# A fused attention and MLP kernel: the last batch's attention in the other direction, MLP weights loaded in other pieces

## The chip, the cores and the metric

One Trainium2 chip, one of its cores. The metric is the device time of one execution in microseconds (us). The kernel before takes 748.22 us, the median of 3 runs (746.31 to 751.43).

## The reference

Three layers follow each other on 4 batches of 768 tokens with 384 channels:

```
state = alpha[t] * state + k[t] v[t]^T ;  y[t] = q[t] state              # gated linear attention, 8 heads of 48
for each of 4 experts e:  a = softmax(causal(q_e k_e^T / 8))             # x = y; q_e, k_e, v_e are x times weights, 64 wide
    out += gate[e] * (a @ v_e) @ wo[e]                                   # gate: softmax over the best two of 4 logits
out + relu(layernorm(out) @ w_ch1) @ w_ch2                               # MLP, 384 -> 1536 -> 384
```

All inputs are fp32. The causal attention of a token block i (128 tokens, i from 0 to 5) looks at i+1 blocks of keys, so the work of a block grows with i.

## The kernel before, in words

The kernel interleaves three strands on the same engines. The **front** (`front`) computes the linear attention in chunks of 128 tokens and the Q, K, V and gates of the second layer. The **attention** of the experts runs in 48 units `u`, listed in `UN`: batch b, token block i, expert pair p, in that order. The **back** (`back`) is the MLP in 12 blocks of 256 tokens: layer norm (`mlp_ln`), transposes (`mlp_tr`), first product (`mlp_1`, 108 matmuls) and second product (`mlp_2`, 72 matmuls).

A loop over the units sets the order: for unit u it issues the transposes of the probabilities (`transp`, L464), the scores two units ahead (`scores`, L432), the product with V (`av`, L487) and, after a pair of units, the output projection (`wout`, L505). Between them, `fill` pulls as much of the front (batches 0 to 2) or of the back (batch 3) as a table of nominal costs says is due. `MB0` (in ns) holds the back's start off by that much nominal work of the last batch. The framework then places the instructions in each engine's own queue, which runs strictly in order.

In `scores`, DVE takes the row maximum (L438 for one half of a wide row, L440 with the causal mask for the rest), ACT makes the exponentials (L442), DVE and POOL make `rr`, the gate over the row sum. In `av`, matmuls of the probabilities with V fill the second 128 columns of a PSUM tile, then two matmuls (L490) spread `rr` over the first 128 columns; ACT copies those (L493, `rb`), DVE multiplies both (L494), ACT and POOL split the result in two parts for `wout`.

The MLP's weights come as 64-bit words (`raw`) and are turned into pairs of fp32r numbers, high and low, by `conv`: a DMA on SP's queue, five operations on DVE (L530 to L534, L544), one on ACT, one on POOL. The first weight is converted in 18 pieces of 256 columns while batches 0 to 2 run, and stored in DRAM (`wsc`). A piece's load waits for a one-element copy on POOL (L526) that reads the latest row maximum; this keeps the load from running far ahead. The load is issued in the same step as the conversion.

At the first unit of the last batch (`u == u3`, unit 36) the front ends and its buffers are freed. `load_mlp(0)` loads the converted first weight, 4.7 MB, from `wsc` by four DMAs of POOL's queue into one tile, in column ranges of the flattened weight. `load_mlp(1)` issues the conversion of all 12 pieces of the second weight (384 columns each, into `w2h` and `w2l`), and `back` starts with the loads of the first two token blocks (`xt`, four DMAs on SP).

Of the kernel before, what the change touches and what calls it, by code (L numbers as in the profile page):

```python
# [11 lines left out]
FR = mybir.dt.float32r  # L12
# [13 lines left out]
MB = 1.0  # L26
MB0 = -15000
TM = 4
# [25 lines left out]
W2 = 384  # L54
PRI = 0
B, H, S, D = 4, 8, 768, 48
DM = H * D
E, HD = 4, 64
DFF = 4 * DM
NSC = S // 128  # L60
KT = DM // 128
# [10 lines left out]
def kernel(ctx: ExitStack, tc: tile.TileContext, akq, vd, wqkv, wo, g_ln, w1, w2, out):  # L72
# [335 lines left out]

    UN = [(b, i, p) for b in range(B) for i in range(NSC) for p in range(2)]
    AA, ATT, OT, RR, M = {}, {}, {}, {}, {}  # L410
# [61 lines left out]
    def av(u):  # L472
# [8 lines left out]
        O = P[:, 128:256]  # L481
        with tc.manual_schedule(engines={mybir.EngineType.PE}):
            for x in range(i + 1):
                for h in range(2):
                    e = 2 * p + h
                    c = 128 * (h * (i + 1) + x)
                    pe.matmul(O[64 * h:64 * h + 64, :], V[:, x, HD * e:HD * e + HD], at[:, c:c + 128],  # L487
                              start=(x == 0), stop=(x == i), skip_group_check=True)
            for h in range(2):
                pe.matmul(P[64 * h:64 * h + 64, :128], rr[:, h:h + 1].to_broadcast([128, 64]), ident, start=True, stop=True,  # L490
                          skip_group_check=True)
        rb = aw.tile([128, 128], F32, name="rb", bufs=2)
# [22 lines left out]
    CW1 = 256  # L515
    NC1 = 3 * DFF // CW1

    def conv(n):
        if n < NC1:
            i, c, cw, p = 0, n, CW1, gw  # L520
        else:
            i, c, cw, p = 1, n - NC1, W2, M["x"]
        cs = slice(cw * c, cw * c + cw)
        raw = p.tile([128, cw, 2], I32, name="raw", bufs=RB)
        if i == 0:
            pool.tensor_copy(raw[0:1, 0, 0:1].bitcast(F32), M["nm"][0:1, 0:1])  # L526
        sp.dma_start(raw.rearrange("p n w -> p (n w)"), (w1, w2)[i][:, 2 * cw * c:2 * cw * (c + 1)])
        a = p.tile([128, cw], I32, name="cva", bufs=CB)
        u = p.tile([128, cw], I32, name="cvu", bufs=CB)
# [18 lines left out]
    def load_mlp(i):  # L548
        if i == 0:
            M["p", 0] = ctx.enter_context(tc.tile_pool(name="mw0", bufs=1))  # L550
            t = M["p", 0].tile([128, 2, 3 * DFF], FR, name="w1hl")
            for c in range(4):
                cs = slice(DFF * 3 // 4 * c, DFF * 3 // 4 * (c + 1))
                pool.dma_start(t[:, :, cs], wsc[:, :, cs])
            for x, n in ((0, "h"), (1, "l")):
                M[f"w1{n}"] = t[:, x].rearrange("p (k c) -> p k c", k=KT)
        else:
# [3 lines left out]
            M["x"] = ctx.enter_context(tc.tile_pool(name="mx", bufs=2))  # L561
            with tc.high_priority(offset=-PRI):
                for c in range(4608 // W2):
                    conv(NC1 + c)

# [51 lines left out]
    def mlp_1(blk, fs):  # L617
        nh, nl = M["n", blk]
        for ff in fs:
            P = psm()[:, :256]  # L620
            c = slice(128 * ff, 128 * ff + 128)
            n = 0
            for w, x in ((M["w1h"], nh), (M["w1l"], nh), (M["w1h"], nl)):
                for k in range(KT):
                    pe.matmul(P, w[:, k, c], x[:, k], start=(n == 0), stop=(n == 8))  # L625
                    n += 1
# [24 lines left out]
    def back():  # L651
        mlp_load(0)
        mlp_load(1)
        mlp_ln(0)
        yield from mlp_tr(0)
        for blk in range(NBLK):
# [7 lines left out]
            if blk + 2 < NBLK:  # L664
                while 256 * (blk + 3) > prog["x"]:
                    yield -1
                mlp_load(blk + 2)
# [42 lines left out]
    for u in range(nu):  # L710
# [13 lines left out]
        if u < u3:  # L724
            ncv = max(0, min(NC1, (NC1 * (u + 1 - CV0)) // (CVU - CV0)))
            while prog["cv"] < ncv:
                conv(prog["cv"])
                prog["cv"] += 1
# [80 lines left out]
```

## Time and profile before

| | |
|---|---|
| median of 3 runs | 748.22 us (746.31 to 751.43) |
| the profiled execution, its own time | 750.77 us |
| its span, first to last instruction | 749.1 us |
| mean granted TensorE clock | 0.973 |
| PE busy | 711.3 us (95%) |
| DVE busy | 448.4 us (60%) |
| ACT busy | 309.2 us (41%) |
| POOL busy | 172.9 us (23%) |

Reading: the span is one execution; 750.77 us is its time as the runs are timed, 1.7 us more than the span. The busy shares are means over very different stretches. From about 472 us on only the MLP is left, and PE runs matmuls back to back; before that the three strands share all engines. A matmul's bar ends when its result is out, which is later than the time at which the next can start, so PE's busy share is too high wherever matmuls of different kinds follow each other.

### The profile page before, as it was taken

What the parts mean: (1) busy time and instruction counts of PE and PEld (TensorE: products, weight loads), DVE (VectorE), ACT (ScalarE), POOL (GpSimd) and SP (SyncE); (2) the same over time, 40 slices, a digit from 0 to 9 for tenths busy, and PEclk for the clock granted to TensorE, in tenths of its full rate; (3) what the DMA queues carried; (4) which work ended last, traced back from release to release, by engine and by line L of the source; (5) the groups of instructions that cost most, each with busy time, mean ns of one, the idle gap of its engine ahead of it and who ended that gap; (6) DMA issues with size and microseconds to landing.
All of it is one profiled execution on the core that took longest, in us unless ns stands there. A gap on an engine that the chain in (4) does not pass through costs nothing.

```text
span 749.1 us, 16235 instructions
## 1 busy us (share of the span) xinstructions
PE 711.3 (95%) x6520; PEld 641.5 (86%) x6520; DVE 448.4 (60%) x1241; ACT 309.2 (41%) x879; POOL 172.9 (23%) x284
## 2 busy tenths in 40 slices
PE   7489799989989899999899999999999999999998
PEld 6478678778868788878677889999999999999997
DVE  6766778767887787766578873254245325433521
ACT  3333455444555555545567553232223123212310
POOL 4643344343554234321233220000000000000000
PEclk9698999989989999999999999999999999999999
DMA  8122423233323612211923311001101100110100
GB/s 338 71 96 90 138 85 135 83 117 122 121 97 96 208 49 92 79 40 55 326 100 95 86 33 62 15 31 43 43 11 33 43 22 22 43 43 12 32 22 22
DMA packets 28380, 60.87 MB, mean 81 GB/s; under 512 B 2961, under 2 KB 16785, under 8 KB 28305
## 3 DMA queue, kind: packets, MB, share of 16 engines
q1 hardware_dynamic: 18864, 45.68, 18.5%
q10 hardware_dynamic: 8352, 9.44, 3.5%
q0 software_dynamic: 1088, 4.72, 1.7%
q8 instruction: 51, 0.84, 0.5%
q14 instruction: 25, 0.20, 0.1%
HBM read 45.67 MB, written 14.16 MB: 80 GB/s over the span
## 4 chain that ended last, share of the span: by engine, by line
PE 59%; DVE 4%; DMA 3%; ACT 2%; POOL 2%; issue 2%; ACTq 0%; POOLq 0%; DVEq 0%
PE F L625 21%; PE F L642 20%; PE F L487 4%; PE F L464 3%; PE F L432 3%; DMA raw<-in_w_dram 2%; PE F L304 2%; PE F L505 2%; PE F L606 1%; PE F L318 1%; DMA ld<-in_akq_dram 1%; ACT A L442 1%; PE F L490 1%; DVE gt L199 1%; PE F L263 1%
## 5 line engine op out<-in xcount | busy, mean ns | idle before, releaser
L629 ACT ACTIVATE hh<-F 128x256 fp32r<-128x256 f32 x144 | 55.0, 384 | 199.9 <-PE F L625 198.8
L625 PE MATMUL F<-nh,w1hl 128*128 128x256 f32 x864 | 129.4, 284 | 0.5 <-ACT nh L610 0.5
L625 PEld LDWEIGHTS F<-nh,w1hl 128*128 128x128 f32 x864 | 114.9, 191 | 2.5 <-issue 1.0
L642 PE MATMUL F<-w2h,hh 128*128 128x384 f32 x288 | 98.1, 341 | 0.0
L642 PE MATMUL F<-w2l,hh 128*128 128x384 f32 x288 | 97.1, 337 | 0.0
L642 PE MATMUL F<-w2h,hl 128*128 128x384 f32 x288 | 96.8, 336 | 0.0
L630 DVE SCALAR_TENSOR_TENSOR hl<-F,hh 128x256 fp32r<-128x256 f32 x144 | 60.0, 420 | 54.2 <-ACT hh L629 54.1
L442 ACT ACTIVATE A<-F,nm 128x384 f32<-128x384 f32 (+4 forms) x128 | 68.5, 542 | 53.5 <-DVE nm L440 43.0
L646 DVE TENSOR_TENSOR xt<-F,xt 128x384 f32<-128x384 f32 x24 | 13.4, 558 | 113.0 <-PE F L642 113.0
L625 PE MATMUL F<-nl,w1hl 128*128 128x256 f32 x432 | 75.7, 283 | 0.0
L487 PE MATMUL F<-at,V 128*64 128x128 f32 x672 | 62.7, 287 | 2.0 <-DVE rb L494 0.9
L625 PEld LDWEIGHTS F<-nl,w1hl 128*128 128x128 f32 x432 | 62.2, 192 | 0.2 <-issue 0.2
L464 PE MATMUL F<-ident,A 128*128 128x128 f32 x336 | 56.1, 289 | 3.1 <-DVE rb L494 2.4
L487 PEld LDWEIGHTS F<-at,V 128*64 128x64 f32 x672 | 41.8, 138 | 18.9 <-issue 7.0
L642 PEld LDWEIGHTS F<-w2h,hh 128*128 128x128 f32 x288 | 54.2, 188 | 0.4 <-issue 0.4
L642 PEld LDWEIGHTS F<-w2l,hh 128*128 128x128 f32 x288 | 54.2, 188 | 0.3 <-DVE at L469 0.2
L642 PEld LDWEIGHTS F<-w2h,hl 128*128 128x128 f32 x288 | 54.1, 188 | 0.0
L464 PEld LDWEIGHTS F<-ident,A 128*128 128x128 f32 x336 | 38.4, 145 | 13.2 <-issue 5.7
L221 PE MATMUL F<-ld 48*128 48x128 f32 x384 | 36.6, 302 | 11.2 <-issue 7.8
L221 PEld LDWEIGHTS F<-ld 48*128 48x128 f32 x384 | 29.3, 197 | 17.3 <-issue 12.0
L206 POOL TENSOR_TENSOR ld<-ld,gt 128x512 f32<-128x512 f32 (+1 forms) x26 | 30.2, 1165 | 59.7 <-DVE gt L199 27.9
L199 DVE TENSOR_TENSOR_SCAN gt<-ld,hot 128x516 f32<-128x516 f32 (+1 forms) x26 | 31.1, 1204 | 16.1 <-DMA ld<-in_akq_dram 12.9
(185 smaller groups left out, 1425.6 us busy)
## 6 DMA issues: line engine op xcount, KB each, us to landing
ld<-in_akq_dram SPq DMA_DIRECT2D x24, 770.0 KB, 5.3
vb<-in_vd_dram SPq DMA_DIRECT2D x24, 256.0 KB, 2.8
raw<-in_w_dram SPq DMA_DIRECT2D x18, 256.0 KB, 2.7
wsc<-whl ACTq DMA_DIRECT2D x18, 256.0 KB, 2.4
xs<-xo ACTq DMA_DIRECT2D x24, 192.0 KB, 1.9
w1hl<-wsc POOLq DMA_DIRECT2D x4, 1152.0 KB, 13.8
raw<-in_w_dram SPq DMA_DIRECT2D x12, 384.0 KB, 3.3
xt<-xs SPq DMA_DIRECT2D x24, 192.0 KB, 2.5
```

The costliest lines, as they stand in the source:

```text
L199: dve.tensor_tensor_scan(gt[:, js].rearrange("p j t -> p (j t)"), al[:, 129 * j0:129 * j1], hot[:, js].rearrange("p j t -> p (j t)"), 0.0, ...
L206: (dve if GQ else pool).tensor_tensor(q[:, js], q[:, js], gt[:, js, 1:], op=OP.mult)
L221: pe.matmul(P[h][:, j], k[r, j], q[r, j], start=True, stop=True)
L304: pe.matmul(P[:, mt % 2], wt[:, k, cs], x[:, k], start=(n == 0), stop=(n == 8))
L432: pe.matmul(P[h][x], qt[rs[h], p, qs], kt[rs[h], p, pw * x:pw * x + pw], start=(n == 0), stop=(n == 2), skip_group_check=True)
L442: act.activation(A[h][:, pw * x:pw * x + pw], t, AF.Exp, bias=nm[:, h:h + 1], scale=1.0 if x < npc - 1 else -1.0, accum_out=dn2[:, h, x:x ...
L464: pe.transpose(P[:, 128 * n:128 * n + 128], A[h][:, 128 * x:128 * x + 128], ident)
L487: pe.matmul(O[64 * h:64 * h + 64, :], V[:, x, HD * e:HD * e + HD], at[:, c:c + 128], start=(x == 0), stop=(x == i), skip_group_check=True)
L625: pe.matmul(P, w[:, k, c], x[:, k], start=(n == 0), stop=(n == 8))
L629: act.activation(hh, P, AF.Relu)
L630: dve.scalar_tensor_tensor(hl, P, 0.0, f(hh), op0=OP.max, op1=OP.subtract)
L642: pe.matmul(P, x[:, o], w[:, ff], start=(ff == 0 and n == 0), stop=(ff == KF - 1 and n == 2))
```

## The change

- The last batch's units run from block 5 down to block 0 instead of from 0 up to 5. Batches 0 to 2 are as before.
- `MB0` goes from -15000 to -10000: the back starts earlier in nominal work.
- In `av` the two matmuls that spread `rr` are issued ahead of the product with V.
- `conv` is cut in two: `conv_load(n)` asks for a piece, `conv(n)` converts it. The load of piece n+1 is issued ahead of the conversion of piece n.
- The second weight's 12 pieces are no longer issued all at unit 36; `CR = 5` issues them at 2.5 pieces a unit over units 37 to 41.
- The `xt` loads of the first two token blocks are issued ahead of the second weight's first piece.
- The first weight goes into four tiles, each with the 384 columns that three steps of `mlp_1` need of all row groups; a DMA's contiguous run is 1536 bytes instead of 4608.

```diff
-MB0 = -15000
+MB0 = -10000
-PRI = 0
+CR = 5
-    UN = [(b, i, p) for b in range(B) for i in range(NSC) for p in range(2)]
+    UN = [(b, i, p) for b in range(B) for i in (range(NSC) if b < B - 1 else reversed(range(NSC))) for p in range(2)]
...
         with tc.manual_schedule(engines={mybir.EngineType.PE}):
+            for h in range(2):
+                pe.matmul(P[64 * h:64 * h + 64, :128], rr[:, h:h + 1].to_broadcast([128, 64]), ident, start=True, stop=True,
+                          skip_group_check=True)
             for x in range(i + 1):
...
-            for h in range(2):
-                pe.matmul(P[64 * h:64 * h + 64, :128], rr[:, h:h + 1].to_broadcast([128, 64]), ident, start=True, stop=True,
-                          skip_group_check=True)
...
+    def conv_load(n):
+        i, c, cw, p = piece(n)
         raw = p.tile([128, cw, 2], I32, name="raw", bufs=RB)
         if i == 0:
             pool.tensor_copy(raw[0:1, 0, 0:1].bitcast(F32), M["nm"][0:1, 0:1])
         sp.dma_start(raw.rearrange("p n w -> p (n w)"), (w1, w2)[i][:, 2 * cw * c:2 * cw * (c + 1)])
+        M["raw", n] = raw
+
+    def conv(n):
+        i, c, cw, p = piece(n)
+        cs = slice(cw * c, cw * c + cw)
+        raw = M.pop(("raw", n))
...
-            t = M["p", 0].tile([128, 2, 3 * DFF], FR, name="w1hl")
+            src = wsc.rearrange("p x (k c) -> p (x k) c", k=KT)
             for c in range(4):
-                cs = slice(DFF * 3 // 4 * c, DFF * 3 // 4 * (c + 1))
-                pool.dma_start(t[:, :, cs], wsc[:, :, cs])
...
+                t = M["p", 0].tile([128, 2, KT, DFF // 4], FR, name=f"w1hl{c}")
+                pool.dma_start(t.rearrange("p x k c -> p (x k) c"), src[:, :, DFF // 4 * c:DFF // 4 * (c + 1)])
+                M["w1", c] = t
...
-            with tc.high_priority(offset=-PRI):
-                for c in range(4608 // W2):
-                    conv(NC1 + c)
+            mlp_load(0)
+            mlp_load(1)
+            conv_load(NC1)
...
-                while 256 * (blk + 3) > prog["x"]:
+                while (256 * (blk + 3) if blk < 3 * S // 256 - 2 else B * S) > prog["x"]:
...
             while prog["cv"] < ncv:
-                conv(prog["cv"])
+                n = prog["cv"]
+                if n + 1 < NC1:
+                    conv_load(n + 1)
+                conv(n)
                 prog["cv"] += 1
+            if u == 0:
+                conv_load(0)
+        else:
+            nc2 = min(NC2, (u - u3) * CR // 2)
+            while prog["cv"] < NC1 + nc2:
+                n = prog["cv"]
+                if n + 1 < NC1 + NC2:
+                    conv_load(n + 1)
+                conv(n)
                 prog["cv"] += 1
```

SP's queue where the last batch begins, before (512 columns of `raw` are a piece of the first weight, 768 one of the second; `xt` is a token block):

```order
L112 DMA vb_89<-in_vd_dram 128x512
L527 DMA raw<-in_w_dram 128x512 x5
L527 DMA raw<-in_w_dram 128x768 x2
L573 DMA xt<-xs 128x384 x4
L527 DMA raw<-in_w_dram 128x768 x10
L647 DMA out_dram<-xt 128x384 x2
```

and now:

```order
L112 DMA vb_89<-in_vd_dram 128x512
L527 DMA raw<-in_w_dram 128x512 x4
L578 DMA xt<-xs 128x384 x4
L527 DMA raw<-in_w_dram 128x768 x12
L653 DMA out_dram<-xt 128x384 x2
```

The four `xt` loads have moved ahead of the second weight's first two pieces, and the last piece of the first weight is asked for earlier, ahead of rows that are not shown.

DVE's queue at the scores of unit 34 (L438 and L440 with 384 columns), before:

```order
L438 TENSOR_REDUCE mx_5018<-F 128x1 x2
L440 ISA F,nm<-F,cmask,mx_5018 128x384
L440 ISA nm 128x1
L440 ISA F,nm<-F,cmask,mx_5018 128x384
L440 ISA nm 128x1
L530 TENSOR_SCALAR cva<-raw 128x384
L531 SCALAR_TENSOR_TENSOR cva<-raw,cva 128x384
L532 TENSOR_SCALAR cvu<-cva 128x384
L534 SCALAR_TENSOR_TENSOR cvu<-raw,cvu 128x384
L338 TENSOR_REDUCE rank<-gt__4997 128x8
L446 SCALAR_TENSOR_TENSOR den<-dn_5019 128x2
```

and now (L590 is the layer norm's statistics of `xt`):

```order
L438 TENSOR_REDUCE mx_5018<-F 128x1 x2
L590 BN_STATS bs<-xt 128x6
L440 ISA F,nm<-F,cmask,mx_5018 128x384
L440 ISA nm 128x1
L440 ISA F,nm<-F,cmask,mx_5018 128x384
L440 ISA nm 128x1
L590 BN_STATS bs<-xt 128x6
L591 BN_AGGR mv<-bs 128x2 x2
L592 TENSOR_SCALAR ve<-mv 128x2
L446 SCALAR_TENSOR_TENSOR den<-dn_5019 128x2
L449 RECIPROCAL den<-den 128x2
```

The conversion of the second weight's first piece stood behind unit 34's masks; its place is now behind the first half of unit 35's, and two of the four statistics of `xt` stand among unit 34's operations, the first ahead of its masks.

PE's queue at the back's first transposes (`ident,xn`), before (L432 with 320 columns are the scores of a block 4, of unit 44):

```order
L505 MATMUL F<-OWH,ol 128x384
L464 MATMUL F<-ident,A 128x128
L487 MATMUL F<-at,V_1411 64x128 x3
L464 MATMUL F<-ident,A 128x128 x4
L606 MATMUL F<-ident,xn 128x128 x6
L432 MATMUL F<-KH_1409,QH_1407 128x320
```

and now (512 columns: the scores of a block 3, of unit 40):

```order
L484 MATMUL F<-ident,rr 64x128 x2
L490 MATMUL F<-at,V_1414 64x128
L611 MATMUL F<-ident,xn 128x128 x6
L490 MATMUL F<-at,V_1414 64x128 x11
L631 MATMUL F<-nh,w1hl_5329 128x256
L464 MATMUL F<-ident,A 128x128 x4
L631 MATMUL F<-nh,w1hl_5329 128x256
L432 MATMUL F<-KH_1412,QH_1410 128x512 x2
```

Before, the back starts ahead of unit 44's scores, when blocks 0 to 2 of the last batch are done; now it starts ahead of unit 40's, at the product of unit 37, the second of block 5.

## Rows read from the trace of the kernel before

**Rows 1.** The page, busy time of engines: busy us, share, instructions.

```profile
PE 711.3 (95%) x6520; PEld 641.5 (86%) x6520; DVE 448.4 (60%) x1241; ACT 309.2 (41%) x879; POOL 172.9 (23%) x284
```

**Rows 2.** Busy time by stretch; clock, DMA share and GB/s at the end.

```profile
357.00:400.00 43.00, 40.33 (x340) 29.71 (x340) 31.38 (x123) 28.96 (x94) 13.53 (x29) 0.96 0.58 198
400.00:432.00 32.00, 31.33 (x268) 27.06 (x266) 27.51 (x79) 20.76 (x66) 9.67 (x14) 1.00 0.34 93
```

**Rows 3.** The chain of waits, 357 us on: start us, us, what.

```profile
357.05 1.06 PE F L432 x7
...
399.85 0.22 PE F L606 x2
...
432.20 1.06 PE F L642 x6
...
472.85 12.48 PE F L642 x72
485.33 12.94 PE F L625 x108
```

**Rows 4.** The chain's shares by line, stretch 200 to 360 us.

```profile
by line: DMA raw<-in_w_dram 11.6%; PE F L304 9.9%; issue 7.4%; PE F L487 5.4%; PE F L432 5.3%; PE F L318 4.7%; PE F L464 4.2%; DMA ld<-in_akq_dram 4.1%; ACT A L442 3.5%; DVE gt L199 3.3%; PE F L263 2.5%; PE F L221 2.2%; PE F L505 2.1%; POOL
```

**Rows 5.** DVE at L530: the group, then three in time with idle before them.

```profile
L530 DVE TENSOR_SCALAR cva<-raw 128x256 int32<-128x256 int32 x18 | 5.8, 325 | 13.3 <-DMA raw<-in_w_dram 13.2
...
301.50 0.29 DVE L530 TENSOR_SCALAR cva<-raw 128x256 int32<-128x256 int32 x1 [0.93 <-DMA raw<-in_w_dram]
...
312.07 0.29 DVE L530 TENSOR_SCALAR cva<-raw 128x256 int32<-128x256 int32 x1 [1.17 <-DMA raw<-in_w_dram]
...
324.87 0.29 DVE L530 TENSOR_SCALAR cva<-raw 128x256 int32<-128x256 int32 x1 [0.91 <-DMA raw<-in_w_dram]
```

**Rows 6.** Waits of DVE at L494: us in total, times, longest.

```profile
DVE rb L494 <- ACT rb L493: 10.1, 10, 2.5
```

**Rows 7.** DVE in time, where the last batch's loads begin; idle before in brackets.

```profile
358.74 0.62 DVE L440 CUSTOM_DVE_ANT_0 F<-F,cmask,mx 128x384 f32<-128x384 f32 x1
...
363.40 0.36 DVE L530 TENSOR_SCALAR cva<-raw 128x384 int32<-128x384 int32 x1 [3.44 <-DMA raw<-in_w_dram]
...
367.03 0.61 DVE L440 CUSTOM_DVE_ANT_0 F<-F,cmask,mx 128x384 f32<-128x384 f32 x1
...
368.58 0.56 DVE L585 BATCH_NORM_STATS2 bs<-xt 128x6 f32<-128x384 f32 x1 [0.65 <-DMA xt<-xs]
...
376.20 0.56 DVE L585 BATCH_NORM_STATS2 bs<-xt 128x6 f32<-128x384 f32 x1 [1.54 <-DMA xt<-xs]
```

**Rows 8.** PE in time, the same place.

```profile
367.10 0.66 PE L464 MATMUL F<-ident,A 128*128 128x128 f32 x4 [1.90 <-DVE rb L494]
```

**Rows 9.** Issue to landing of the four xt loads, then of the first weight's.

```profile
DMA to landing us min/median/max: 9.6/11.9/15.4
...
DMA to landing us min/median/max: 8.0/13.8/19.5
```

**Rows 10.** ACT and DVE groups of a unit and of a piece, by shape.

```profile
L467 ACT ACTIVATE at<-F 128x512 f32<-128x512 f32 x52 | 31.1, 599 | 5.4 <-PE F L464 4.1 <-DVE smk L225 1.1
L442 ACT ACTIVATE A<-F,nm 128x384 f32<-128x384 f32 x48 | 27.6, 584 | 16.1 <-DVE nm L440 14.2 <-PE F L318 1.4 <-PE F L464 0.4
L442 ACT ACTIVATION_READ_ACCUMULATOR A<-F,nm 128x1 f32 x128 | 25.9, 203 | 0.0
L495 ACT ACTIVATE oh<-rb 128x128 fp32r<-128x128 f32 x48 | 14.8, 308 | 22.5 <-DVE rb L494 22.2 <-ACT at L467 0.2
L493 ACT ACTIVATE rb<-F 128x128 f32<-128x128 f32 x48 | 13.2, 275 | 23.9 <-PE F L490 14.9 <-PE F L221 2.6 <-DVE whl L544 2.4
...
L534 DVE SCALAR_TENSOR_TENSOR cvu<-raw,cvu 128x384 f32<-128x384 uint32 x12 | 7.7, 645 | 0.3
```

**Rows 11.** The chain, PE's pace in two kinds of matmul.

```profile
407.96 0.91 PE F L487 x13
...
426.77 1.05 PE F L505 x6
```

More of the change, by code (lines that the diff above doesn't have):

```diff
@@ L516, with piece @@
     NC1 = 3 * DFF // CW1
[L518 to L523, printed above, removed]
+    NC2 = 3 * DFF // W2
+    def piece(n):
+        return (0, n, CW1, gw) if n < NC1 else (1, n - NC1, W2, M["x"])
+    def conv_load(n):
+        i, c, cw, p = piece(n)
         raw = p.tile([128, cw, 2], I32, name="raw", bufs=RB)
@@ L550, in load_mlp @@
             M["p", 0] = ctx.enter_context(tc.tile_pool(name="mw0", bufs=1))
-            t = M["p", 0].tile([128, 2, 3 * DFF], FR, name="w1hl")
+            src = wsc.rearrange("p x (k c) -> p (x k) c", k=KT)
             for c in range(4):
-                cs = slice(DFF * 3 // 4 * c, DFF * 3 // 4 * (c + 1))
-                pool.dma_start(t[:, :, cs], wsc[:, :, cs])
-            for x, n in ((0, "h"), (1, "l")):
-                M[f"w1{n}"] = t[:, x].rearrange("p (k c) -> p k c", k=KT)
+                t = M["p", 0].tile([128, 2, KT, DFF // 4], FR, name=f"w1hl{c}")
+                pool.dma_start(t.rearrange("p x k c -> p (x k) c"), src[:, :, DFF // 4 * c:DFF // 4 * (c + 1)])
+                M["w1", c] = t
         else:
@@ L620, in mlp_1 @@
             P = psm()[:, :256]
-            c = slice(128 * ff, 128 * ff + 128)
+            t = M["w1", ff // 3]
+            c = slice(128 * (ff % 3), 128 * (ff % 3) + 128)
             n = 0
-            for w, x in ((M["w1h"], nh), (M["w1l"], nh), (M["w1h"], nl)):
+            for w, x in ((t[:, 0], nh), (t[:, 1], nh), (t[:, 0], nl)):
                 for k in range(KT):
@@ L651, in back @@
     def back():
-        mlp_load(0)
-        mlp_load(1)
         mlp_ln(0)
@@ L726 @@
             while prog["cv"] < ncv:
-                conv(prog["cv"])
+                n = prog["cv"]
+                if n + 1 < NC1:
+                    conv_load(n + 1)
+                conv(n)
+                prog["cv"] += 1
+            if u == 0:
[7 more added lines that the diff above has]
+                conv(n)
                 prog["cv"] += 1
```

## The prediction

> **What bounds the kernel now.** I read the page's engine totals first: PE is busy 95% of the span [rows 1], so only what PE loses can be won. From 472.85 us on nothing is lost: 72 matmuls take 12.48 us and 108 take 12.94 us [rows 3], 173 and 120 ns each, one behind the other to the end. No part of the change touches that tail but the order of two weight tiles. So I looked at the stretches before it, by busy time [rows 2], and then at the chain of waits for the moments at which the last batch begins (unit 34's scores, 357.05 us), the back begins (399.85 us), its second product begins (432.20 us) and block 2 begins (485.33 us) [rows 3].
>
> The stretch from 357 to 400 us is the loose one: PE starts only 340 matmuls in 43 us, 126 ns each where many are short products that can follow each other every 70 ns (0.91 us for 13) [rows 2, 11], and no other engine is above 31.4 us [rows 2]. Something waits there that is no engine's throughput. DVE's rows in time show it: unit 34's mask starts at 358.74, then DVE stands 3.44 us for the first piece of the second weight, starts unit 35's mask at 367.03 only, and stands again for `xt` at 368.58 and at 376.20 [rows 7]. PE pays with a hole of 1.90 us [rows 8], and the granted clock of the stretch is 0.96 [rows 2], so part of it ran at the lower of TensorE's two levels. From 400 to 432 us DVE is busy 27.5 of 32 us [rows 2]: there it is the bound.
>
> **The change, part by part.** The sum is made against the profiled execution, 750.8 us, which is 2.55 us above the median of the runs; what it gains is taken off the median of 748.2.
>
> *Pieces of the first weight asked for ahead.* DVE waits 13.2 us for these loads in all [rows 5]; the chain from 200 to 360 us has 11.6% of its time, 18.6 us, on such loads [rows 4], but that is issue to landing, and the load's own time is mostly covered. What removal can give is DVE's idle time where the chain passes. It passes five pieces of the first weight there (and the second weight's first at its end); in three of them DVE stood 0.93, 1.17 and 0.91 us [rows 5], in the other two little. That is 3.0 us; the other 10 us of DVE's waiting lie where PE had other work. I take 3.0; the ends are 0, if POOL or PE is late next, and 13.2. SP's queue has each piece's place moved one piece earlier and no other load behind a later wait, so the front's own loads cost nothing more.
>
> *`rr` spread ahead of the product.* The instructions are the same, so PE's work is the same. The rule that speaks against a gain is visible in the built program: ACT's copy of the spread `rr` (275 ns [rows 10]) still waits for the last matmul of the product, not for the spread itself. So DVE's 10.1 us of waiting for that copy [rows 6] stays, but for the two short matmuls that no longer stand between product and copy. Those move out of the tail into the time in which PE waits for the copied probabilities. I take 1.0 us over 48 units, with 0 and 3.4 (a third of the 10.1) as ends. The Trainium skill says why the copy cannot start early: its page PSUM — Partial Sum Buffer, section "PSUM bank collisions raise a hardware error", asks that two engines be kept apart by bank, and both halves of this tile share one. By that page the gain of an early copy is nil; without it, up to the 10.1 us would be the term.
>
> *The last batch from long to short, and the back earlier.* Between unit 34's scores and the back's first transposes PE now issues 72 score matmuls, 64 transposes, 57 products for each pair's two halves, 12 spreads and 18 projections; before, 72, 68, 65, 18 and 30. So 12 projections of 177 ns (1.05 us for 6), 16 half products of 70 ns and a few spreads and transposes, about 4.4 us of PE work, move behind that point [rows 11]. What the new stretch lasts I price by ACT, which the wide units load most. A wide unit has four exponentials of 584 + 203 ns, three copies of which three in four are ACT's at 599 ns, and 275 + 308 ns around the product [rows 10]. Six units' exponentials are 18.9 us, 64 transposes make 16 copies, 12 of them ACT's, 7.2 us, and 5.5 units' small operations 3.2 us: 29.3 us. To that I add 5 us for waits on loads that remain. `xt` now lands ahead of the second weight's first piece, and DVE stands for it at unit 34's masks, then for that piece in the middle of unit 35's; before, the shown waits of the same kind were 3.44, 0.65 and 1.54 us [rows 7], 5.6 in all. So the back begins some 34.3 us after unit 34's scores, not 42.8: 8.5 us earlier. Less the 4.4 us of PE work that now come later, 4.1 us are won. The ends: 29.3 us, ACT never waiting, a gain of 9.1 us; and 42.8 us as before, where the late work makes it a loss of 4.4 us.
>
> *The pieces of the second weight* are spread over units 37 to 41. They cost DVE the same; one operation alone is 645 ns [rows 10]. Half of the stretch that DVE bounds is this work, before and now, because the back starts with two pieces done instead of four, six fall into the first product in both, and four instead of two into the second. I take 0 with 2 us to either side. Of the two more in the second product: unit for unit the 72 matmuls of 173 ns and the narrow units beside them take as long as DVE needs for them, so again 0, and 3 us at worst.
>
> *Weight tiles by steps of the first product.* The load has three times as many runs, of 1536 bytes; a quarter of the weight suffices to begin. The load lands 8.0 to 19.5 us after issue [rows 9], that is before 380 us, and the first product begins after 390: nothing, and at worst 1 us.
>
> The sum: -3.0 - 1.0 - 4.1 = -8.1 us, 742.7 for the profiled execution and **740 us** for the median.
>
> **The rivals.**
>
> *Nothing comes of it.* The wide units without MLP work beside them have long waits of their own: scores, row maximum, mask, exponentials, transposes in turn, each on another engine. For it speaks that before, ACT was busy 29.0 of the 43 us in this stretch [rows 2] and the bound was still not ACT; if the same share holds, 29.3 us of work take 43 again. Then the last batch gives -4.4 back to +4.4 us, the front's 4.0 us cancel it: 748.6 us. Against it speaks that 5.6 us of the old stretch were waits for loads.
>
> *The whole loose stretch closes.* ACT is the bound at 29.3 us (gain 9.1), the front gives 6 us because the waits off the chain count too, and 2 more come from the narrow units under the second product: 731 us. For it speaks that PE has work from three units at any time; against it that each engine's queue is strict.
>
> *Slower: the `xt` loads hold DVE.* DVE's mask of unit 34, which all later exponentials need, is now queued behind a statistic of `xt`. Before, the four `xt` loads took 9.6 to 15.4 us from issue to landing beside the first weight's 4.7 MB [rows 9], and DVE reached the last only at 376.20 [rows 7]. If they land as late now, unit 35's masks wait until about 376, not 367.03: 9 us on the stretch instead of the 8.5 us won, so +0.5, +4.4 of late PE work, -4.0 from the front, and about 3 us for a longer hole in PE at the lower clock: 752 us. It decides from the point at which the last `xt` lands later than about 370 us. Against it speaks that in the old order two pieces of 384 KB stood ahead of `xt` in SP's queue, and that in the new one the first `xt` is issued as soon as the front's last matmul is done.
>
> **How the numbers follow.** A measurement of this kernel can tell about 1% from no change, so the borders are 740.7 and 755.7 us. The forecast (735 to 744 us) has a chance of 0.53, three in five of it below 740.7; nothing (744 to 751) 0.24; the loose stretch closing (727 to 735) 0.14; slower (751 to 760) 0.09, half of it above 755.7. The range of 728 to 752 us takes in the best ends of the last batch's and the front's terms (-9.1, -9, -2 us) and the worst (+4.4 and 0); it leaves out about one in ten. Faster 0.47, the same 0.48, slower 0.05.
>
> **What would show it.** In the changed kernel's chain the first-weight loads should be gone from the front, and the first operation of a conversion (L536 there) should not wait for DMA. From unit 34's scores to the back's first transposes I expect 34 us (30 to 38), with DVE's statistics of `xt` waiting 1 to 3 us each at most and the first unit's mask done within 5 us of its scores. DVE should be busy nearly 90% in the first product. L494's wait for ACT should stay near 10 us. From the back's first transposes to block 2 I expect 90 us against 85.5 (485.33 less 399.85). I would be wrong if the front's end, the last scores of batch 2, came more than 6 us earlier or not at all; if the wide units took 7 us each; or if PE stood for the second weight at L648.

## The result: 0.55% slower, not 1.1% faster

The changed kernel takes 753.98 us (median of 7 runs, 751.58 to 756.36) against 748.22 us for the kernel before (7 runs on the same chip): ratio 1.0055, 95% interval 1.0029 to 1.0081. The forecast was 740 us, the range 728 to 752. The two profiled executions lie nearer together than the medians, 752.12 and 750.77 us; the profiled one of before was a long one, that of the change a short one. A cause can therefore not be read from these two traces alone.

The page of the changed kernel, engine totals, answers to [rows 1]:

```profile
PE 714.0 (95%) x6520; PEld 643.2 (86%) x6520; DVE 448.7 (60%) x1241; ACT 309.0 (41%) x879; POOL 173.6 (23%) x284
```

Busy time by stretch in the changed kernel answers to [rows 2]. The stretches are those between the front's last projection (L318), the back's first transposes, block 0's second product and block 2.

```profile
359.80:395.20 35.40, 33.79 (x296) 26.14 (x294) 25.48 (x92) 23.49 (x77) 8.46 (x18) 1.00 0.70 201
395.20:422.90 27.70, 27.01 (x242) 23.94 (x242) 24.45 (x69) 17.17 (x51) 9.09 (x13) 1.00 0.36 101
422.90:486.50 63.60, 63.60 (x465) 55.84 (x464) 33.47 (x107) 27.25 (x84) 10.84 (x19) 1.00 0.16 51
```

The chain of waits of the changed kernel, 357 us on, answers to [rows 3]:

```profile
358.98 1.10 PE F L318 x9
361.43 6.85 DMA xt<-xs
369.70 0.65 PE F L464 x4
...
423.19 1.22 PE F L648 x7
...
474.20 12.48 PE F L648 x72
486.68 3.34 PE F L631 x28
```

The front ends 3 us later (360.1 against 357.05), though the forecast took 4 us off it. From there the back begins after 35.4 us instead of 42.9, the second product begins 9 us earlier, counted from the start of the program (423.19 against 432.20), and then the gain is given back: block 2 begins at 486.7, 1.4 us later than before. From there to the last matmul both take 260.3 us.

DVE's waits in the changed kernel (us in total, times, longest), for [rows 5, 6]:

```profile
DVE rb L494 <- ACT rb L493: 16.8, 16, 2.6
DVE cva L536 <- DMA raw<-in_w_dram: 15.0, 13, 2.5
...
DVE bs L590 <- DMA xt<-xs: 11.8, 13, 1.8
```

Neither wait that the front's two edits were aimed at became shorter: 15.0 us for the first weight's pieces (13.2 before), 16.8 for the copy of `rr` (10.1 before).

### The profile page after: what moved, and what is told of

Same layout as the page of the kernel before. It is cut to its first block, busy times and chain, and to the rows that moved or that the text cites. A ratio compares the mean times of both kernels' runs of the same rounds, so it can differ in the third digit from the quotient of the medians.

```text
span 750.4 us, 16245 instructions
## 1 busy us (share of the span) xinstructions
PE 714.0 (95%) x6520; PEld 643.2 (86%) x6520; DVE 448.7 (60%) x1241; ACT 309.0 (41%) x879; POOL 173.6 (23%) x284
## 4 chain that ended last, share of the span: by engine, by line
PE 73%; DVE 8%; DMA 6%; ACT 3%; issue 2%; POOL 2%; SPq 0%; ACTq 0%; DVEq 0%; POOLq 0%
PE F L631 21%; PE F L648 20%; PE F L304 6%; PE F L490 4%; DMA ld<-in_akq_dram 4%; PE F L432 4%; PE F L464 4%; PE F L263 3%; PE F L505 3%; DVE gt L199 2%; PE F L318 2%; PE F L484 2%; PE F L221 2%; PE F L244 1%; DMA raw<-in_w_dram 1%
## 5 line engine op out<-in xcount | busy, mean ns | idle before, releaser
L490 PE MATMUL F<-at,V 128*64 128x128 f32 x672 | 59.5, 280 | 0.7 <-ACT at L467 0.7
L490 PEld LDWEIGHTS F<-at,V 128*64 128x64 f32 x672 | 43.7, 137 | 7.7 <-issue 2.1
L199 DVE TENSOR_TENSOR_SCAN gt<-ld,hot 128x516 f32<-128x516 f32 (+1 forms) x26 | 31.1, 1203 | 16.4 <-DMA ld<-in_akq_dram 13.2
```

The source lines that it names most:

```text
L199: dve.tensor_tensor_scan(gt[:, js].rearrange("p j t -> p (j t)"), al[:, 129 * j0:129 * j1], hot[:, js].rearrange("p j t -> p (j t)"), 0.0, ...
```

## The experiments

18 kernels ran. The ratio is to the kernel before on the same chip. Single runs of the kernel before scatter by over 10 us, and most of that goes with the mean granted clock of the run (the column "clock" has its mean): over 141 of its runs the span falls by 5.0 us per 0.01 of clock, and a straight line through them leaves 1.3 us. So the table has a third reading, the mean distance in us of a kernel's spans from that line at their own clocks ("equal clock", with its standard error). It is a second look and not the measure: the line is one for all chips, and on the single chips the kernel before itself lies from -0.7 to +0.4 us off it; and if an edit's own holes on PE lower the clock, this reading leaves that cost out.

| kernel | median us | ratio (95%) | clock | equal clock |
|---|---|---|---|---|
| change | 753.98 | 1.0055 (1.0029-1.0081) | .973 | +4.3 ± 0.5 |
| rr_alone | 756.54 | 1.0071 (1.0047-1.0096) | .970 | +4.4 ± 0.5 |
| ahead_alone | 747.36 | 0.9972 (0.9949-0.9996) | .975 | -1.0 ± 0.4 |
| last_alone | 750.26 | 1.0011 (0.9978-1.0045) | .972 | +0.8 ± 0.6 |
| after_no_rr | 748.91 | 0.9981 (0.9953-1.0008) | .974 | -0.3 ± 0.3 |
| ahead_held | 746.84 | 0.9976 (0.9946-1.0006) | .974 | -0.9 ± 0.5 |
| rr_front | 754.71 | 1.0058 (1.0035-1.0082) | .967 | +3.2 ± 0.5 |
| rr_lastb | 751.71 | 1.0034 (1.0002-1.0065) | .974 | +4.2 ± 0.3 |
| rr_mid | 753.66 | 1.0050 (1.0023-1.0078) | .971 | +3.8 ± 0.6 |
| rr_own | 759.20 | 1.0154 (1.0120-1.0188) | .971 | +8.9 ± 0.3 |
| pace_last | 745.28 | 0.9944 (0.9914-0.9974) | .977 | -2.3 ± 0.4 |
| pace_first | 750.14 | 1.0031 (0.9998-1.0064) | .973 | +2.1 ± 0.4 |
| dve_last | 754.08 | 1.0034 (1.0006-1.0062) | .969 | +1.7 ± 0.3 |
| dve_first | 760.37 | 1.0113 (1.0077-1.0148) | .970 | +9.1 ± 0.5 |
| rr_but8 | 751.85 | 1.0054 (1.0033-1.0076) | .969 | +1.0 ± 0.7 |
| last_fwd | 748.49 | 0.9993 (0.9963-1.0023) | .973 | -1.1 ± 0.5 |
| last_xtback | 746.98 | 0.9963 (0.9938-0.9989) | .976 | -0.2 ± 0.5 |
| pace_ahead | 745.21 | 0.9919 (0.9892-0.9945) | .977 | -2.2 ± 0.3 |
| best2 | 748.55 | 0.9998 (0.9977-1.0019) | .976 | +0.3 ± 0.4 |

### Each part alone

rr_alone is the kernel before with the change's hunk of av() alone. ahead_alone is the kernel before with the hunk of the first weight alone:

```diff
-                conv(prog["cv"])
+                n = prog["cv"]
+                if n + 1 < NC1:
+                    conv_load(n + 1)
+                conv(n)
...
+            if u == 0:
+                conv_load(0)
```

A hunk is one connected piece of a diff. last_alone is the changed kernel with both of these hunks undone, after_no_rr the changed kernel with the hunk of av() undone.

> The kernel before with one edit: the two matmuls that spread rr stand ahead of the product. Theory A (the front's own parts cost time: the chip's 3 us in the front come from rr, because PE now meets rr, which needs the exponentials' sums, DVE's reciprocal and POOL's product, before it may start the product, where before the product covered that): 749 to 751.5 us, 1 to 3 us above the kernel before; PE's idle time just ahead of the spread 8 us or more, where before it was none. Rival B (the prediction's term: the tail behind the product is shorter): 747.2 us, 1 us below, and DVE's wait for ACT's copy 1 to 3 us less. Rival C (nothing comes of it, the front's 3 us are from the pieces asked for ahead): within 0.5 us of the kernel before.

> The kernel before with one edit: each piece of the first weight is asked for one piece ahead of its conversion. Reading of the built program: the conversion of piece n+1 now stands in DVE's queue where that of piece n stood, so load and conversion moved together by one piece. Theory A (so nothing is won): 748.2 us, within 1 us; DVE waits at the first operation of the conversions 12 to 17 us in all, as before (13.2, with the second weight's first piece 16.7), 0.2 to 2.7 us each. Rival B (the prediction's term): 745 us, 3 us below, and these waits under 5 us. Rival C (one more piece's load beside the front's own loads delays them): 750 to 751.5 us, 2 to 3 us above.

> The changed kernel with its two edits in the front undone (the spread behind the product again, each piece of the first weight loaded just ahead of its conversion); the last batch from long to short, its xt loads first, the second weight's pieces spread, and the first weight's four tiles stay. Theory A (the front lost 3 us by its own two edits, the last stage won 2 to 4): front's last projection at 357 us after the start as before, and 744.5 to 746.5 us. Rival B (the front is no slower than before by these edits, and the whole is the last batch's doing): 751 to 754 us, as the changed kernel. Rival C (the last batch as predicted, 4.1 us won): 744 us.

> The changed kernel with the spread of rr behind the product again; pieces of the first weight asked for ahead and the whole last batch stay. If the three parts add up (spread +5.3, pieces ahead -2.1, last batch +0.8 us): 748 to 749.5 us, level with the kernel before. If the spread cost only in company with the other parts of one of them: 751 us or more. If the prediction's other terms hold once the spread is gone (-7.1): 741 to 743 us.

The parts add up: +0.71 - 0.28 + 0.11 = +0.54%, and the whole is +0.55%. The spread ahead of the product is the whole loss; the pieces ahead give some 2 us; the last batch gives nothing, with its interval from -1.7 to +3.4 us. Taking the spread out of the change makes it level (0.9981). ahead_alone lies between its theory A and its rival B in time, with the waits of theory A (13.0 us at the first weight's pieces). last_alone, level with the kernel before, met none of its three. For rr_alone theory A had the direction right, not the size (1 to 3 us expected, 5.3 measured) and not the reason: PE does not stand 8 us ahead of the spread. By the profile's waits it stands 1.6 us ahead of the spread (L484, two waits for ACT), and in the kernel before it stood 2.0 us ahead of the product (L487).

### Why asking ahead gave little

In the built program the conversions moved with their loads. In the changed kernel the timeline has the first two loads (SP) and conversions (DVE) so:

```profile
58.35 0.33 SPq L527 DMA_DIRECT2D raw<-in_w_dram  x1
62.46 0.30 DVE L536 TENSOR_SCALAR cva<-raw 128x256 int32<-128x256 int32 x1 [1.74 <-DMA raw<-in_w_dram]
70.48 0.33 SPq L527 DMA_DIRECT2D raw<-in_w_dram  x1
73.45 0.28 DVE L536 TENSOR_SCALAR cva<-raw 128x256 int32<-128x256 int32 x1
```

and in the kernel before:

```profile
71.27 0.33 SPq L527 DMA_DIRECT2D raw<-in_w_dram  x1
75.77 0.34 DVE L530 TENSOR_SCALAR cva<-raw 128x256 int32<-128x256 int32 x1
85.50 0.33 SPq L527 DMA_DIRECT2D raw<-in_w_dram  x1
88.21 0.29 DVE L530 TENSOR_SCALAR cva<-raw 128x256 int32<-128x256 int32 x1 [1.31 <-DMA raw<-in_w_dram]
```

2.7 to 4.5 us lie between load and conversion in both; the train of 18 pairs has moved by one piece. ahead_held keeps the conversion where it was:

```diff
         u = p.tile([128, cw], I32, name="cvu", bufs=CB)
+        if i == 0:
+            pool.tensor_copy(a[0:1, 0:1].bitcast(F32), M["nm"][0:1, 0:1])
```

> As the kernel before with the pieces of the first weight asked for ahead, and besides each conversion held back where it stood: POOL writes one element of the conversion's buffer from the row maxima of the latest scores, 18 copies of 0.17 us, so DVE may not begin it a piece earlier. Load and conversion are then a whole piece apart. Theory A (the prefetch gained nothing only because the conversion moved with the load): the wait at the conversions of the first weight falls from 13.2 to under 3 us, and the time by up to 3 us, 745 to 747.5 us. Rival B (these waits lie beside PE's work anyway, the chain only passes them): the waits fall likewise, and the time stays at 748.2, within 1 us. Rival C (the hold itself costs, POOL's queue waits for the maxima): 749 us or more.

Now DVE has no wait for a piece of the first weight. The only one at this line is for a piece of the second:

```profile
DVE cva L538 <- DMA raw<-in_w_dram: 0.6, 1, 0.6
```

The time is that of ahead_alone (746.84 and 747.36 us), where the waits stayed at 13.0 us. By its number theory A is met too (745 to 747.5 us), but the same time came with the waits, so their removal is not what won it. In this the runs side with rival B: DVE's waits for the pieces lie beside PE's work, and removing all of them is worth nothing that can be measured. DVE stands elsewhere instead: its waits for the copy of `rr` are 21.7 us in ahead_held, 14.3 in ahead_alone. Where ahead_alone's 2 us come from, if they are more than scatter, is open.

### Where the spread costs

rr_front and rr_lastb are rr_alone with the spread ahead only where u < u3 (units 0 to 35), and only from there on. rr_mid has the spread behind the product's first block of keys (`if x == 0` inside the product's loop). rr_own is rr_alone with

```diff
         O = P[:, 128:256]
+        Q = psf()[:, :128]
...
-                pe.matmul(P[64 * h:64 * h + 64, :128], rr[:, h:h + 1].to_broadcast([128, 64]), ident, start=True, stop=True,
+                pe.matmul(Q[64 * h:64 * h + 64, :], rr[:, h:h + 1].to_broadcast([128, 64]), ident, start=True, stop=True,
...
-        act.activation(rb, P[:, :128], AF.Copy)
+        act.activation(rb, Q, AF.Copy)
```

> The kernel before with the spread of rr ahead of the product in units 0 to 35 (batches 0 to 2) and behind it in the last 12. rr_alone was 5.3 us above the kernel before (ratio 1.0071, 1.0047 to 1.0096), and at equal mean granted clock 4.4 us. Theory A (each unit pays about 0.09 us for the new order, 4.4 us by 48): 36 units, 3.3 us, 752.5 to 753.5 us. Rival B (the cost arises in the last batch, where no front work covers a wait): within 0.7 us of the kernel before. Rival C (no cost of the order itself: the other built order of the instructions happened to be worse): any time from 747 to 754 us, and rr_front and rr_lastb do not add up to rr_alone.

> The kernel before with the spread of rr ahead of the product in the last 12 units alone. Theory A (0.09 us a unit): 1.1 us above the kernel before, 750 to 751.5 us. Rival B (the cost arises in the last batch): 753 to 755 us. Rival C (chance of the built order): not 5.3 us less what rr_front costs.

> The kernel before with the spread of rr between the product's first block of keys and the others: the unit's block on PE begins with a product matmul, as before, and ends with one, as in the change. Theory A1 (the cost comes from the block's head: PE meets rr first, and the scheduler places the block by rr's readiness): as the kernel before, within 1 us. Theory A2 (the cost comes from the block's end: ACT's copy, DVE's multiplication and POOL's rest now hang on the product's last matmul with nothing behind it): 4 to 5.5 us above the kernel before. Rival C (chance of the built order): neither is bound to come out.

> The kernel before with the spread ahead of the product and in a PSUM buffer of its own, so ACT's copy of it waits for the spread alone and DVE's multiplication for the product alone: what the change could have meant. Theory A (the spread ahead costs by what it moves on DVE and PE, and a copy that still waits for the product gives nothing back): with the copy freed DVE's wait for it falls from 10 us to under 4, ACT's wait for PE ahead of the copy from 15 to under 5, and the time is 748 to 751 us, less than rr_alone's 754 to 756. Rival B (the spread ahead of the product costs by itself, whoever waits): 754 us or more. Rival C (the prediction's bound, the copy's wait was worth its third): 745 to 747 us.

rr_mid does not compute the layer: the spread's start flag falls into the middle of the product's sum in the same bank, and the first block of keys is probably left out (argued, not shown); the instructions are the same, and its time counts. All four are slower. So the loss is not that of one batch alone: rr_front costs 0.58%, rr_lastb 0.34%, together more than the 0.71% of rr_alone (rival C). It is not the block's head either (theory A1), since rr_mid begins with the product. Theory A2, the block's end, is not excluded: rr_mid stands 0.50%, 3.7 us, above, where A2 forecast 4 to 5.5. In rr_own ACT's copy is free of the product, and the time rises twice as far, so the copy's wait was not a price. (rr_own also takes one more PSUM buffer a unit; how much of its loss is that was not tried.) What DVE waits for has mostly changed its name:

```profile
DVE rb L495 <- PE F L491: 11.4, 9, 5.3
```

### The order itself, or the luck of one order

Two pairs, each of the kernel before with one edit, and in the one named first besides the spread ahead of the product: pace_first and pace_last, dve_first and dve_last. rr_but8 is rr_alone with the spread behind in units 7 to 11.

```diff
-PF1 = 0.98
+PF1 = 0.979
```

```diff
-        pool.tensor_tensor(rr, den, W[:, i, 2 * p:2 * p + 2], op=OP.mult)
+        dve.tensor_tensor(rr, den, W[:, i, 2 * p:2 * p + 2], op=OP.mult)
```

> The kernel before with the front's pace constant PF1 at 0.979 instead of 0.98, the spread behind the product: no instruction is added, only the built order changes, 207 of 5194 instructions of PE and 173 of 1243 of DVE stand elsewhere. rr_alone moved 484 and 302 of them. Theory A (the spread ahead of the product costs, not the reordering as such): within 1.5 us of the kernel before. Rival B (the kernel before sits on a lucky order, and any reordering of this size costs what rr_alone cost): 3 to 6 us above.

> As pace_last, with the spread ahead of the product. Theory A: 4 to 6 us above pace_last, as rr_alone stands to the kernel before. Rival B (lucky order): level with pace_last within 1.5 us, whether that is slow or not.

> The kernel before with the spread ahead of the product, and rr multiplied by DVE right behind its reciprocal instead of by POOL: 48 small operations of about 0.17 us more on DVE, one engine less between the exponentials' sums and PE. Theory A (PE meets rr too early, and rr's lateness is POOL's): level with dve_last within 1.5 us. Rival B (the order costs whoever makes rr, by the order the scheduler builds): 4 to 5.5 us above dve_last.

> The kernel before with rr multiplied by DVE and the spread behind the product as before: the partner of dve_first. Theory A and rival B alike: 747 to 751 us, since rr is needed last there and DVE gains 8 us of small work over 360 us in which it is three quarters busy.

> rr_alone (the kernel before with the spread ahead of the product, +5.3 us) with the spread behind the product in units 7 to 11 alone; up to about 210 us the built order of DVE is then that of the kernel before. Theory A (the bulk of the cost is the holes of units 8 to 11, PE standing for masks and for rr): 750.5 to 752.5 us, 2 to 4 us less than rr_alone, and no hole of over 1 us on PE ahead of the masks' users at 150 to 160 us. Rival B (the cost is spread evenly over 48 units, a few tenths of a microsecond at many places): 43 of 48 units, 754 to 755.5 us.

A change of pace alone, which moves 207 of PE's instructions, made the kernel 0.56% faster, which neither theory A nor rival B of pace_last had: a built order can be worth some 4 us by itself. But four pairs that differ in the spread alone stand 0.71, 0.74, 0.87 and 0.79% apart (rr_alone, the change, pace, dve), 5.3 to 6.5 us, always the same way. It is not POOL's lateness with `rr` either: dve_first is no nearer to dve_last. (dve_last itself is 0.34% slower than the kernel before, where both theories had it level; why was not looked into.)

The traces of the pairs show a part of where. DVE in time in pace_last, about unit 11's multiplication L494:

```profile
187.85 0.68 DVE L308 SCALAR_TENSOR_TENSOR QL<-F,QH 128x512 fp32r<-128x512 f32 x1
188.45 0.67 DVE L205 SCALAR_TENSOR_TENSOR ld<-ld 128x512 f32<-128x512 f32 x1
189.05 0.28 DVE L494 TENSOR_TENSOR rb<-F,rb 128x128 f32<-128x128 f32 x1
189.25 0.41 DVE L469 COPY at<-F 128x256 f32<-128x256 f32 x1
189.58 1.27 DVE L225 TENSOR_TENSOR smk<-F,gmask 128x512 f32<-128x512 f32 x2
```

and in pace_first:

```profile
186.91 0.68 DVE L205 SCALAR_TENSOR_TENSOR ld<-ld 128x512 f32<-128x512 f32 x1
187.94 0.29 DVE L494 TENSOR_TENSOR rb<-F,rb 128x128 f32<-128x128 f32 x1 [0.35 <-ACT rb L493]
188.43 0.69 DVE L308 SCALAR_TENSOR_TENSOR QL<-F,QH 128x512 fp32r<-128x512 f32 x1 [0.20 <-ACT QH L307]
189.04 0.41 DVE L469 COPY at<-F 128x256 f32<-128x256 f32 x1
189.37 1.28 DVE L225 TENSOR_TENSOR smk<-F,gmask 128x512 f32<-128x512 f32 x2
```

With the spread ahead, the built order puts the multiplication ahead of the front's L308; its operand is not there, and DVE, which works its queue strictly in order, stands with the front's work behind it. PE's timeline, two projections of the front around that place, pace_last then pace_first:

```profile
174.07 0.63 PE L318 MATMUL F<-WH,xh 128*128 128x260 f32 x3
...
198.98 0.52 PE L318 MATMUL F<-WH,xh 128*128 128x260 f32 x3
```

```profile
173.12 0.63 PE L318 MATMUL F<-WH,xh 128*128 128x260 f32 x3
...
198.72 0.52 PE L318 MATMUL F<-WH,xh 128*128 128x260 f32 x3
```

24.91 and 25.60 us: 0.69 lost. The kernel before and the change have 24.89 and 25.60 there (172.98 to 197.87, 172.15 to 197.75). The granted clock of this stretch is 1.00 in every trace. Something similar is seen at unit 8: PE's waits from 139 to 170 us in dve_first,

```profile
PE F L263 <- DVE rb L494: 1.6, 1, 1.6
PE F L464 <- DVE smk L225: 1.4, 1, 1.4
PE F L484 <- ACT A L442: 1.1, 1, 1.1
PE F L505 <- ACT A L442: 0.8, 1, 0.8
PE F L432 <- DVE rb L494: 0.7, 1, 0.7
PE F L304 <- DVE st L254: 0.3, 1, 0.3
```

against those in dve_last:

```profile
PE F L432 <- ACT at L467: 2.0, 1, 2.0
PE F L505 <- ACT A L442: 0.8, 1, 0.8
```

5.9 us against 2.8. In four of the six PE waits for DVE, for the multiplication or for masks and states; in one, 1.1 us, it stands ahead of the spread, for the exponentials from which `rr` comes. The change and after_no_rr have 6.3 and 3.4 us here, the pace pair 5.3 and 5.2. Not all of this need be the order's: dve_last and after_no_rr ran part of the stretch at the lower clock (0.89 against 1.00), and a slower PE may wait less.

In the order of DVE's queue I then counted, for each of the 36 units of batches 0 to 2, how many of the front's own DVE instructions (lines below 405) stand ahead of the unit's multiplication, and took the difference to the partner without the edit. A place earlier is one such instruction that now stands behind the multiplication:

```
kernel (partner)            places earlier in all   units
ahead_alone (before)         0                      none
rr_lastb (before)            0                      none
ahead_held (before)          6 (and 1 later)        8, 15, 17, 22, 25 (later: 19)
rr_but8 (before)             4                      21, 32
the change (after_no_rr)     6 (and 1 later)        8, 11, 21 (later: 32)
rr_alone (before)            7                      8, 11, 21, 32
rr_front (before)            7                      8, 11, 21, 32
rr_mid (before)              7                      8, 21, 32
pace_first (pace_last)       5                      8, 11, 21
dve_first (dve_last)         8                      8, 11, 16, 17, 21
rr_own (before)             28                      15 units
```

The kernels with the spread ahead in these units have 4 to 8 places and lose 0.5 to 0.9%, rr_own has 28 and loses 1.5%. But the count does not give the loss: ahead_held has 6 places and loses nothing, and rr_lastb has none and loses 0.34%.

All 20 traces side by side show how far the account holds. Between the two projections about unit 11, 25.60 us pass in each of the six kernels whose multiplication moved there (the change, rr_alone, rr_front, rr_own, pace_first, dve_first). Of the other 14, twelve, rr_mid among them, have 24.88 to 24.93; ahead_held has 25.13 and rr_but8 25.38. So at unit 11 a loss of 0.7 us goes with the place, and not with the spread as such. Between the projections about unit 21 (272.02 to 295.83 in the kernel before, granted clock 1.00 in all) the six kernels with three places moved there take 0.4 to 1.0 us longer than their partners, but rr_mid and rr_own, with four, lose at most 0.2. These two stretches are 1.1 to 1.7 us of the 5.3 to 6.5; unit 8 may add some.

The rest is not explained, and rr_lastb shows that part of it has another place. Its multiplications in the front stand where they stood; its loss comes behind the front. From the front's last projection to block 2, in rr_lastb and then in the kernel before:

```profile
353.60:485.60 132.00, 127.44 (x1000) 107.51 (x999) 84.03 (x267) 68.63 (x211) 28.94 (x50) 0.99 0.32 102
356.76:485.20 128.44, 125.10 (x1000) 106.23 (x999) 83.61 (x267) 68.36 (x211) 28.95 (x50) 0.99 0.32 104
```

132.0 us against 128.4 at the same clock, and most of the multiplications that moved among the MLP's instructions on DVE stand later there, not earlier. What costs time in the last batch is open.

rr_but8 lies between A and B: 0.54% by its ratio, and +1.0 us at equal clock, +1.7 against the kernel before's own runs on its chip, where rr_alone has +4.4. What was not tried is the repair: the spread ahead with the multiplication held at its old place.

### The last batch

last_fwd is after_no_rr with the units of the last batch from short to long again, MB0 = -15000, and the later `xt` loads waiting for their own token blocks as in the kernel before. last_xtback is after_no_rr with

```diff
-            mlp_load(0)
-            mlp_load(1)
             conv_load(NC1)
...
     def back():
+        mlp_load(0)
+        mlp_load(1)
         mlp_ln(0)
```

> after_no_rr (748.9 us, ratio to before 0.9981) with the last batch from short to long again and MB0 at -15000; its xt loads, the second weight's spread pieces and the four tiles stay. Theory A (the reversal wins 3 to 4 us in the stretch behind the front and pays as much later, so it is worth nothing): 748 to 750 us. Rival B (the reversal is what holds the last batch level, the spread pieces and the early xt loads cost): 751 to 754 us. Rival C (the reversal costs, the other parts win): 744 to 747 us.

> after_no_rr (748.9 us) with the xt loads of blocks 0 and 1 issued where the kernel before had them, behind the second weight's first pieces, at the back's start. Theory A (the early xt loads hold DVE 1 to 7 us at the third batch's end, and so took back part of the stretch's gain): 745 to 747.5 us, PE's hole after unit 34's scores under 1.5 us. Rival B (what ends the stretch is ACT and PE in the wide units, not xt): 748 to 750 us. Rival C (xt then comes too late for the back's first transposes): 750 to 752 us, the back's first transposes 2 us later or more.

The reversal is worth nothing: forward 0.9993, reversed 0.9981. The early `xt` loads are worth nothing that can be told either: 0.9963 without them. In last_fwd the back begins 39.8 us after the front's last projection and block 2 another 85.4 us later; in after_no_rr it is 34.9 and 91.1: 4.8 us won, 5.7 paid.

### The two parts that did not cost, on the better pace

pace_ahead is ahead_alone with PF1 = 0.979, best2 is last_xtback with PF1 = 0.979.

> The kernel before with PF1 at 0.979 (pace_last: 745.3 us, ratio 0.9944) and the pieces of the first weight asked for ahead (ahead_alone: ratio 0.9972). If the two add up: 743 to 744.5 us. If each was the luck of one built order, the sum tells nothing of the parts: 745 to 751 us.

> last_xtback (746.98 us, ratio 0.9963: the changed kernel without the spread first and with the xt loads at the back's start) with PF1 at 0.979. If the better pace (ratio 0.9944 alone, 0.9919 with the pieces asked for ahead) and the last batch's order add up: 742 to 744.5 us. If the last batch's order is worth nothing: 744.5 to 746 us, level with pace_ahead. If the built orders do not combine: 747 us or more.

pace_ahead is the best of all, 745.21 us, ratio 0.9919 (0.9892 to 0.9945): faster than the kernel before and the change. By the ratio its two parts add up (0.9944 times 0.9972 is 0.9916); at equal clock it stands where pace_last does (-2.2 and -2.3 us), so what the pieces ahead add is not shown. best2, which has the better pace with the last batch's order, has lost all of that (0.9998): gains of built orders need not add.

## Why the prediction was wrong, by its steps

The prediction had named its own sign of being wrong, that the front ends no earlier than before: it ended 3 us later.

- **Pieces ahead, -3.0: size nearly right, reason wrong.** -2.1 us (-0.3 to -3.8), which is luck as far as the reason goes. The step failed where it said that SP's queue moves each piece one place earlier and stopped there; DVE's queue moved as well, so the load was never ahead. And the wait's removal, in ahead_held, bought nothing: a wait on the chain of waits was taken for a price, while beside it PE had work or stood for something else. (The range's best end takes 9 us for the front, though the ends given for its two terms are 13.2 and 3.4; the miss was at the other end.)
- **`rr` first, -1.0 with 0 as its worst end: the failed step.** It measured +5.3 to +6.5 us. "The instructions are the same, so PE's work is the same" held, and so did the rule that the copy still waits for the product: freeing the copy (rr_own) gave no gain at all. What the step left out is that the order of all other instructions is built anew around the moved two. I bounded a gain and named no reason that excludes a loss. What the runs show in its place: with the multiplication placed too early on DVE 0.7 us are lost at unit 11, and in most of these kernels 0.4 to 1.0 about unit 21; where the rest of the loss arises, the part in the last batch above all, stays open.
- **Last batch, -4.1: nothing, +0.8 us (-1.7 to +3.4).** The new stretch was forecast at 34.3 us and took 35.4; from the back's first transposes to block 2, 90 us were forecast and 91.3 came. The mis-sized term is the base: 42.8 us came from one profiled execution, with 3.4 us of it at the lower clock; the same short-to-long order, with other edits and in one execution each, takes 40.8 us in pace_last, 39.8 in last_fwd and 38.9 in ahead_alone. A gain of 4.8 us instead of 8.5 does not pay for the PE work moved behind it, forecast at 4.4 us and measured at 5.7 (last_fwd against after_no_rr).
- **Second weight's pieces and the four tiles, 0.** Nothing speaks against it: from block 2 to the last matmul it is 260.3 us in both. They were not tried apart.
- **The slower rival had nearly the right time and the wrong cause, which is luck.** It named 752 us for `xt` loads that hold DVE. DVE in time in the changed kernel, for [rows 7]:

```profile
362.53 0.56 DVE L590 BATCH_NORM_STATS2 bs<-xt 128x6 f32<-128x384 f32 x1 [0.68 <-DMA xt<-xs]
363.01 0.61 DVE L440 CUSTOM_DVE_ANT_0 F<-F,cmask,mx 128x384 f32<-128x384 f32 x1
...
368.30 0.56 DVE L590 BATCH_NORM_STATS2 bs<-xt 128x6 f32<-128x384 f32 x1 [0.75 <-DMA xt<-xs]
...
369.63 0.62 DVE L440 CUSTOM_DVE_ANT_0 F<-F,cmask,mx 128x384 f32<-128x384 f32 x1
```

The last `xt` is there at 368.3 us, before the 370 from which the rival was to decide; the chain runs through these loads (6.85 us of it), yet DVE stands 1.4 us for them, and last_xtback, without them, is no slower. It is the second entry of a chain here that is no price.

## What to carry to other kernels

Where a scheduler builds the queues, an edit that moves an instruction earlier can move what depends on it too: before pricing it, compare the built order of every engine, and ask of each instruction that moved forward on an in-order queue whether its operand is really there, and what stands behind it. A wait that shows on the chain is not a price until an experiment removes it; and a stretch's length from one execution is not a base when its clock was not that of the others.

## What the runs showed that I had not expected

The spread of a kernel's times goes mostly with the granted clock: 744 to 756 us for the kernel before, 5.0 us per 0.01 of mean clock, 1.3 us of scatter left. Reading the clock of each run beside its span about halves the scatter (from 2.4 to 1.3 us); the kernel before's own runs then still differ by up to 1.2 us from chip to chip.

DVE operations are stretched beside POOL's. In the changed kernel 17 DVE operations took over 0.5 us more than the median of their kind, 13.2 us in all, every one beside a POOL operation; in the kernel before 15 did, 11.8 us. In the timeline of pace_last the same operation on 128x2 takes 0.15 us, and 1.22 us beside POOL's L203:

```profile
183.97 0.15 DVE L448 TENSOR_SCALAR den<-den 128x2 f32<-128x2 f32 x1
...
196.80 1.28 POOL L203 TENSOR_TENSOR ld<-gt,gi 128x512 f32<-128x512 f32 x1
196.89 1.22 DVE L448 TENSOR_SCALAR den<-den 128x2 f32<-128x2 f32 x1
```

The Trainium skill, page SBUF — State Buffer, section "Who interferes with whom", says that DVE in certain modes and POOL share a pair of ports and that the later one blocks for the whole instruction; the trace agrees with these two durations. It is little of the difference between the kernels.
